# A clamp moved from VectorE to GpSimd, waits of GpSimd for VectorE's weight rounding, and another written-out order, in a fused set attention and SwiGLU kernel

## The chip, the cores and the metric

The kernel runs on one core of a Trainium2 chip. The metric is the device time of one execution in microseconds (us). Of several executions the median is taken. One further execution was profiled; its own time is given beside the others. The engines are named as in the profile: PE is TensorE (matrix products), PEld its weight load, DVE is VectorE, ACT is ScalarE, POOL is GpSimd, and SP is the queue that issues most DMAs.

## The reference

The reference is an attention block followed by a gated feed-forward block, all in float32.

```python
# x: (4, 12416, 128)   inducing: (32, 128)
def mab(q, kv):
    s = scale * (q @ kv.transpose(0, 2, 1))
    s = s - s.max(-1, keepdims=True)
    a = np.exp(s)
    a /= a.sum(-1, keepdims=True) + 1e-09
    return a @ kv
h = mab(inducing, x)        # 32 rows a batch
x = mab(x, h)               # 12416 rows a batch
# x as 49664 rows of 128; w_gate, w_val: (128, 1536), w_out: (1536, 128)
rms = np.sqrt(np.mean(x * x, axis=-1, keepdims=True) + 1e-06)
xn = x / rms * rms_g
g = xn @ w_gate
out = (g / (1 + np.exp(-g)) * (xn @ w_val)) @ w_out
```

The three weight matrices come as float64 words in DRAM and are turned into float32 on the chip.

## The kernel before

**Units and blocks.** Each of the 4 batches is cut into 25 units of mostly 512 tokens (some of 480, one of 256). A unit passes through 12 blocks of 128 hidden features, so there are 1200 blocks. A block is a gate product on PE (`gate`, L709), a Silu on ACT (`silu`, L719), a value product on PE (`value`, L737), and a product of the two on DVE (`times_value`, L751). Then the block is projected with `w_out` into a sum in PSUM.

**Three sorts of projection.** A written-out string gives each block a sort. Sort P multiplies the float32 factor directly (`project_plain`, L807: two matmul records a block). Sorts S and D split the factor into a high and a low part, so that three faster products do (`project_two`, L795 and L796, and `project_third`, L807). In sort S, ACT makes the high part (`high`, L764), DVE the low part (`low`, L770) and POOL their sum (`add_in_place`, L815). In sort D, ACT makes the high part (L761), POOL the low part (`low_of_u`, L777), ACT scales the high part (L783), and POOL makes the sum (L815). Before the change 368 blocks are P, 635 S and 197 D.

**Attention beside it.** While the blocks of one batch run, the scores, exponentials and sums of the next one are computed in small steps between them. The rows of a batch are also normed (`norm`): a transpose on DVE (L548), a small product (L562, L569), a product (L574) and a sum of rows on DVE (`scale`, L583), which gives the mean squares `ms`; then `clamp` (L586), a maximum of `ms` and 1e-6 over 8 to 64 numbers a partition; then a first guess of the inverse root on ACT (`seed`, L590), and three rounds of a root iteration, each with two steps on ACT (L594, L600) and two on POOL (L597, L603); then the product of the weights with it on POOL (L608). There are 10 such clamps in the part of the kernel described here. The first set of rows has its own code ahead of it, with its own clamp (L1029) and root (L1032), which the change does not touch.

**Rounding of the weights.** Each of nine chunks of 128 x 512 weights is turned from float64 words into float32 by four DVE steps: `power` (L226) and `upper` (L239), each a shift or mask of one operand in SBUF, and `sign` (L248) and `lower` (L254), each with two operands in SBUF. Two ACT steps lie between (L204, L206), and `join` on POOL (L260) multiplies the parts. Some of these steps run in the opening (`first`, a written-out order of its own), the others among the first blocks, next to the splitting of `w_out` (L666 to L672 on ACT and POOL).

**The order.** Every engine runs its instructions in the order in which the program emits them. That order is a string, `program`, with one letter a step (g, s, v, m for the parts of a block, h, l, n, e, q, d, r, p for its projection), and a dot for one of 871 steps of attention, norm and rounding, whose number is read from a second list, `taken`. Further strings give the PSUM bank (`banks`), the buffers (`workers`, `outputs`, `holders`), the block's sort (`sorts`), and which of several waiting blocks goes next (`picks`). The layer below adds the waits that the data need.

```python
    for name in "".join(program.split()):
        if name == ".":
            step, args = micros[int(next(taken))]
            step(*args)
        else:
            do[name]()
```

Of the kernel before, what the change touches and what calls it, by code (L numbers as in the profile page):

```python
# [14 lines left out]
ALU = mybir.AluOpType  # L15
# [8 lines left out]
def kernel(  # L24
# [501 lines left out]
    def norm(b, sets):  # L526
# [58 lines left out]
        def clamp():  # L585
            nc.vector.tensor_scalar(out=st["ms"], in0=st["ms"], scalar1=1e-6, scalar2=None, op0=ALU.max)  # L586
# [595 lines left out]
    def seams():  # L1182
# [61 lines left out]
        gpmdojlkhqiasncrlpmekqsnobgfjpmrlkdaqsionmrljchekpofnqgsmrkplojbsmnqrkplodajsrcknmqiopjlsknrhmqjflnsebropjgdklan
        msrqocpjikhflqonmpsjrklgmqeopnsdrbalkcjmhiqnsfoprlkqgnsjdoemkaqprlnsjcmonskbrlfqphjmoniasrkqlpjodkgmnseclfbjprko
        qhmsinrlkjpomdgcnljqakrbopesmfjhopincabsmjkqolrndgsmjpfqhelaknbosrmcjqplikrmnjqogpdhfkslrjmanoqpblekcjgrmnsfqljp
        iokqdnhrlsjamopnkqergfcslmjbophankridmqojepslnkromfcgdplkbrsnqjopakhrifclmsngjqeoprkdbljmqsnrokpmaclfijrhgqosnkj
        pmdrlsnqebckorpjmslikqnrhafopjslmkgdqcebnorjlpmsqkniafhldopcmrsjqgnkelobmprqfsljnokhmadpsiglrcbjqefdg
    """
    sorts = """  # L1250
        PPPPPDPPPPPPDPDDPPPSPDDPDPPPDPPDDPPPPPPSSSSDPPDPDPDPPDPSDPPSPSPSSSDPDPPPPSSDSPSDDSSPSSSSDPSSSSSSPSSDPSPSSSSDDSPS
        DSDPSPSSPSSSSSPSDDPSPDSPPDPSPSSPPSPPSSSDDPSPPSSSPDSPSSSDSSPSSSSPSSPSSSSSSSDSDPSPSSPDSDSSPSSSSDSDSDSSSPSPSSPSDSDP
        PPPPSSDSSSSPDPSPSSSSDDPSPPPSPDPDDSPPSDSPPDSSDPPPSPSPPSSSSSPPPPSSDPPSSDDDPPPPDPDDPDPSSDPSPSPDDPSSSPPPSPSSSDDPPPSD
        PSSSDPSPDSPSSPSDSDDSSSPSSSSDDPSPSSSPPSSDDPSSPPSSPDSSSSDSSSPSSPSDPSDSPSPSSSSSDSPSDSSPSSSSSDPPPSSPDSSDPPDSPSPPSPPS
        SDDSPPSSDSSPDPSSSSSDSSPSSSSSPPSSSSSDSSPSSSSSSPSSSDSPSSSSSSDSSSDPSSSSPDSSPDSPSSSPSSDPSSSPSSDPSSPSDPSSPSSPPDSPDDPP
        PPSPDDSPSSSSPSPSPSPPSSPDSPSPPSSPSDSSSPSPDDDPDPSDPSPSDPPSPDSPSDPPSPPSSSDPSPSSSSDSDPSPSPSSSDDSSDPSPSDSSSSPDPDPSSPP
        SDSDSPSSPSPSDSSSPPSSPDSSDDSDPSSSSPDSPSSSSDSSPSSPSSDSPPSPSSSSSDPPDPSDDPPPSPSSPSSDSDPPDSSDPSSSSPSSDSSPPSDSPSSSSSSS
        SDSPSSSPDSSDSSSSSSSDPSSDSSDPSPSSSSPSSSDPPSSPSSSSSSPDSSSPPSDDSSPSDSPPPDPDDPDPPPPPDPDPSSPSSPSPSSPSDPSPPPSPPPPSSSSD
        PSSPSDSSDPSSDPPSDSPSSSSDPSPPSSPSSPPSPSSSPSSSSDSSSSPSSSDSSSSSPSSSPSPSDDSSPSPSPSSSSSSSSPDSDPPSPSSSSSPSSSDSSSSSSSPS
        SSPDSPSSSPSSDSSPSSPSPSSSSDSSDPSPSPSSPSSSSSSDSPSSPSDSSPSPSSSSSPDSSPSSPSSSSSSDSPSSSSPSSSDDPSSPPSPSDSPSSSSSSDPSSSSS  # L1260
        SPDSSPPSSSSSSSSSDSPPSPSSSSDSPSPSSSDSSPSSSSSPSDPSSSSPDPSSPSSSSPSDSSPSSPSPPDPDPPPP
    """
# [225 lines left out]
```

## Time and profile before

| what | value |
|---|---|
| median of three executions | 1492.43 us |
| lowest and highest | 1492.39 and 1493.38 us |
| the profiled execution's own time | 1493.58 us |
| its span in the profile | 1491.8 us |
| granted TensorE clock | 1.00 |

The span is what the profile shows from the first to the last instruction. Busy times of an engine's instructions are merged where they overlap. Matmul ends are modelled, so the distance from one matmul to the next tells more of the pace than its duration.

### The profile page before, as it was taken

How to read it: one execution, taken by the hardware profiler on the slowest of the kernel's cores; microseconds unless marked ns; L12 is line 12 of the kernel's file. 1: busy time of each engine (PE TensorE's matmuls, PEld its weight loads, DVE VectorE, ACT ScalarE, POOL GpSimd, SP SyncE). 2: the span in 40 equal slices, each digit the busy share in tenths (PEclk: the TensorE clock that was granted, in tenths of full speed). 3: DMA queues.
4: the chain of work that ended last, by engine and by line, in shares of the span. 5: the costliest groups of instructions: out<-in, count | busy, mean ns of one | idle time of the engine just before them, and what ended most of it. 6: DMA issues, size and time to landing. Idle time of an engine off the chain costs nothing.

```text
span 1491.8 us, 25915 instructions
## 1 busy us (share of the span) xinstructions
PE 1471.9 (99%) x7280; PEld 1100.2 (74%) x7280; DVE 1431.6 (96%) x2471; ACT 1308.5 (88%) x2603; POOL 1372.0 (92%) x1190
## 2 busy tenths in 40 slices
PE   8899999999999999999999999999999999999998
PEld 6456777767777777777777777777767777787787
DVE  6999998999999999899999999999999999999998
ACT  5798889888988888988999888998898889898987
POOL 1588997999999999899999999989989999999998
PEclk9999999999999999999999999999999999999999
DMA  7576324438553313445755312263332121222122
GB/s 285 113 117 112 64 40 97 87 94 125 101 92 66 57 31 70 87 94 125 118 104 103 74 29 43 43 134 86 76 63 45 29 40 36 42 40 41 36 42 35
DMA packets 391712, 116.28 MB, mean 78 GB/s; under 512 B 365584, under 2 KB 370704, under 8 KB 389008
## 3 DMA queue, kind: packets, MB, share of 16 engines
q1 hardware_dynamic: 390976, 114.55, 39.4%
q8 instruction: 58, 0.95, 0.3%
q14 instruction: 86, 0.70, 0.2%
q10 hardware_dynamic: 592, 0.08, 0.0%
HBM read 53.95 MB, written 27.00 MB: 54 GB/s over the span
## 4 chain that ended last, share of the span: by engine, by line
PE 93%; DVE 3%; issue 1%; ACT 1%; DMA 1%; SPq 0%; POOL 0%; DVEq 0%; ACTq 0%; POOLq 0%
PE gv L807 31%; PE gv L737 17%; PE gv L709 17%; PE gv L795 12%; PE gv L796 12%; PE gv L316 3%; PE gv L369 1%; DVE u L751 1%; PE gv L908 1%; DMA xn<-in_x_dram 1%; PE gv L569 1%; DVE o L254 0%; DVE we L248 0%; DVE we L226 0%; DVE gv L751 0%
## 5 line engine op out<-in xcount | busy, mean ns | idle before, releaser
L719 ACT ACTIVATE silu<-gv 128x512 f32<-128x512 f32 (+2 forms) x1200 | 670.6, 593 | 87.1 <-PE gv L709 61.5
L815 POOL TENSOR_TENSOR xn<-xn,xn 128x512 fp32r<-128x512 f32 (+1 forms) x480 | 596.1, 1259 | 17.0 <-PE gv L796 13.5
L709 PE MATMUL gv<-a,sg 128*128 128x512 f32 (+2 forms) x1188 | 490.8, 440 | 3.8 <-DVE xn L770 1.8
L737 PE MATMUL gv<-a,sv 128*128 128x512 f32 (+2 forms) x1188 | 442.8, 408 | 1.5 <-DVE sv L492 1.0
L751 DVE TENSOR_TENSOR gv<-silu,gv 128x512 f32<-128x512 f32 (+2 forms) x635 | 417.4, 677 | 9.6 <-ACT silu L719 4.5
L764 ACT ACTIVATE xn<-gv 128x512 fp32r<-128x512 f32 (+1 forms) x616 | 362.1, 599 | 38.1 <-DVE gv L751 31.1
L751 DVE TENSOR_TENSOR u<-silu,gv 128x512 f32<-128x512 f32 (+2 forms) x565 | 360.9, 655 | 13.2 <-ACT silu L719 5.9
L807 PE MATMUL gv<-u,wo 128*128 128x512 f32 (+2 forms) x736 | 361.3, 575 | 3.1 <-DVE u L751 3.1
L770 DVE SCALAR_TENSOR_TENSOR xn<-xn,gv 128x512 fp32r<-128x512 f32 (+2 forms) x516 | 337.7, 666 | 6.5 <-ACT xn L764 4.6
L709 PEld LDWEIGHTS gv<-a,sg 128*128 128x128 f32 x1188 | 223.2, 189 | 114.7 <-issue 35.1
L737 PEld LDWEIGHTS gv<-a,sv 128*128 128x128 f32 x1188 | 222.9, 189 | 90.5 <-issue 25.1
L815 POOL TENSOR_TENSOR xn<-xn 128x512 fp32r<-128x512 f32 (+2 forms) x201 | 251.7, 1259 | 12.7 <-PE gv L796 9.8
L777 POOL TENSOR_TENSOR xn<-u,xn 128x512 fp32r<-128x512 f32 (+2 forms) x165 | 206.5, 1257 | 21.5 <-ACT xn L761 19.0
L815 POOL TENSOR_TENSOR u<-xn,u 128x512 fp32r<-128x512 f32 (+2 forms) x131 | 162.9, 1248 | 5.3 <-PE gv L796 2.6
L795 PE MATMUL gv<-xn,xn 128*128 128x512 f32 (+2 forms) x439 | 167.7, 382 | 0.0
L807 PEld LDWEIGHTS gv<-u,wo 128*128 128x128 f32 x736 | 137.0, 190 | 27.0 <-issue 9.6
L807 PE MATMUL gv<-xn,xn 128*128 128x512 f32 (+2 forms) x367 | 141.0, 390 | 0.0
L796 PE MATMUL gv<-xn,xn 128*128 128x512 f32 (+2 forms) x367 | 137.5, 375 | 0.0
L795 PE MATMUL gv<-xn,more 128*128 128x512 f32 (+2 forms) x349 | 135.0, 387 | 0.0
L783 ACT ACTIVATE xn<-xn 128x512 fp32r<-128x512 f32 (+2 forms) x196 | 122.4, 632 | 7.5 <-POOL xn L777 6.4
L761 ACT ACTIVATE xn<-u 128x512 fp32r<-128x512 f32 (+2 forms) x196 | 122.4, 626 | 7.5 <-DVE u L751 5.6
L807 PE MATMUL gv<-xn,more 128*128 128x512 f32 (+2 forms) x302 | 114.7, 391 | 0.0
(223 smaller groups left out, 1818.9 us busy)
## 6 DMA issues: line engine op xcount, KB each, us to landing
out_dram<-o SPq DMA_DIRECT2D x320, 64.0 KB, 2.0
xT<-in_x_dram SPq DMA_DIRECT2D x60, 256.0 KB, 4.9
xn<-in_x_dram SPq DMA_DIRECT2D x60, 256.0 KB, 5.4
a<-hi SPq DMA_DIRECT2D x156, 64.0 KB, 2.0
a<-lo SPq DMA_DIRECT2D x156, 64.0 KB, 2.0
xn<-in_x_dram SPq DMA_DIRECT2D x5, 1024.0 KB, 9.7
xn<-w SPq DMA_DIRECT2D x18, 256.0 KB, 3.8
out_dram<-o SPq DMA_DIRECT2D x64, 60.0 KB, 2.0
```

What stands on the lines that cost most here:

```text
L709: nc.tensor.matmul(g[:, 0:T], stacks[b][0][:, ts(j, P)], halves_in_turn(one["a"][:, 0:T]), start=True, stop=True)
L719: nc.scalar.activation(sl[:, 0:T], gates.pop(n)[:, 0:T], AF.Silu)
L737: nc.tensor.matmul(v[:, 0:T], stacks[b][1][:, ts(j, P)], halves_in_turn(one["a"][:, 0:T]), start=True, stop=True)
L751: nc.vector.tensor_tensor(out=to, in0=sl[:, 0:T], in1=v[:, 0:T], op=ALU.mult)
L761: nc.scalar.activation(hi, t["u"], AF.Copy, scale=1.0 - 2.0 ** -13)
L764: nc.scalar.activation(hi, t["u"], AF.Copy, scale=-(1.0 - 2.0 ** -13) * 2.0 ** -12)
L770: nc.vector.scalar_tensor_tensor(out=t["lo"], in0=t["hi"].bitcast(F32), scalar=4096.0, in1=t["u"], op0=ALU.mult, op1=ALU.add)
L777: nc.gpsimd.tensor_tensor(out=t["lo"], in0=t["u"], in1=t["hi"].bitcast(F32), op=ALU.subtract)
L795: nc.tensor.matmul(to, weight_of(0, j), halves_in_turn(t["hi"]), start=not one["q"], stop=False)
L796: nc.tensor.matmul(to, weight_of(1, j), halves_in_turn(t["lo"]), start=False, stop=last)
L807: nc.tensor.matmul(to.rearrange("p (n h) -> p h n", h=2) if step2 else to, lhsT, rhs, start=one["left"] == NJ, stop=one["left"] == 1)
L815: nc.gpsimd.tensor_tensor(out=t["lo"], in0=t["hi"].bitcast(F32), in1=t["lo"].bitcast(F32), op=ALU.add)
```

## The change

It has three parts.

- The clamp of `norm` (L586) is issued to GpSimd in place of VectorE.
- While the order is emitted, each DVE step of the rounding (`power`, `upper`, `sign`, `lower`) is remembered, and the next GpSimd instruction that is emitted is made to wait for the last of them.
- All the order strings are new: `program`, `taken`, `banks`, `workers`, `outputs`, `holders`, `sorts`, `picks`. The number of blocks and of the 871 small steps is the same. The sorts are now 362 P, 643 S and 195 D. `first` and its order are as before.

```diff
         def clamp():
-            nc.vector.tensor_scalar(out=st["ms"], in0=st["ms"], scalar1=1e-6, scalar2=None, op0=ALU.max)
+            nc.gpsimd.tensor_scalar(out=st["ms"], in0=st["ms"], scalar1=1e-6, scalar2=None, op0=ALU.max)
...
     sorts = """
-        PPPPPDPPPPPPDPDDPPPSPDDPDPPPDPPDDPPPPPPSSSSDPPDPDPDPPDPSDPPSPSPSSSDPDPPPPSSDSPSDDSSPSSSSDPSSSSSSPSSDPSPSSSSDDSPS
+        PPPPPPPPPPPPPDDDPPPSPDPPDPPDPDPSSDPPDPDPPDPPPPPSDDDPDPDPSPSPSDPDSSPPPPSSPSSSSDSPSDPSSPDSSSSSSSDPSPSDDPSSPSPSDPSD
...
+    held = None
+    alone = {id(one[name]) for one in weight.values() for name in ("power", "upper", "sign", "lower")}
     for name in "".join(program.split()):
-        if name == ".":
-            step, args = micros[int(next(taken))]
-            step(*args)
-        else:
-            do[name]()
+        made = len(nc.cur_bb.bb.instructions)
+        step, args = micros[int(next(taken))] if name == "." else (do[name], ())
+        step(*args)
+        one = nc.cur_bb.bb.instructions[-1]
+        if id(step) in alone:
+            held = one
+        elif held is not None and one.engine == mybir.EngineType.Pool and len(nc.cur_bb.bb.instructions) > made:
+            tc.add_manual_dep(one, held.name, mybir.DependencyInfo(mybir.DependencyClass.Sync, mybir.DependencyReason.DATA),
+                              reason="no two at the shared port")
+            held = None
```

More of the change, by code (lines that the diff above doesn't have):

```diff
@@ new lines @@
+        7426543172632516730257156701350357064317064306247604062475027064571427015701537414213547231472513467541350463150
+        4135046530241564363016430176301746301724630716207516205321056310261405631574316371536741670456306751067102652057
+        2570126507142571245714235174271354270643276345276527346275327464152364526345324502643056413206415027561207561057
+        6120376253172142674561426541270564217045720437142741037126407236257342653475367264157637164314017360713604137607
+        4153756345315215634160254310523104571230451204750416205421602364013503052413547032451724657142637162314761234712
@@ new lines @@
+        3467123061421325614532426756053075620562357230167501653176417534675671362457214235120321370157312510367250617564
+        6246041712160421736230173616071561637601563075643764532645234256325143521463251305402503254234720472536420736027
+        3464167462061270416071521050616521063215031025463152603176031635071736051630154702432124157134512745163721641206
+        4236143613260413670326470260237052670325710263517253237543154713273561247623407636270612071023610256751467251462
+        5176514725641357613615617036710536057167102571271470254724107521460152403514325431423014250145301504305450370457
@@ new lines @@
+        6302456730245632431206523026312560712037614261013071437201357240153425304614620136014620132014327345207354037540
+        2354673046215406215046510265402650264765072673250632753604327453715052054517420714756210425601352103210650263501
+        7653145075065351375061750537215403140537120142307203142031643127532654512435625142305364502347052367327642576324
+        7321437250437524375240732605413251427141346124361724173062413602410536140351406351436547065203405306524502340267
+        3402640230634026413062167403641036401351463514056734256741265243124631623562041354163257435731516547635016741571
@@ new lines @@
+        2056215625460216452130420643274320436076204753264357614213471362376423016720472014564152420641205340263275602475
+        2760574025176254637251372457143152307451204715276510761026517365023640576042734350423754210753702132370210726135
+        2071362073462130143061402134561042615067156215427546172534526134063456145601634507645174607462071274126702671347
+        0360135017673617536072361251725374327341534752362145362341301503520450137243031702310612067032613760521705620412
+        7405170124073517354014607436746574053764052364721307063710726317503274052374062032764271603274026703653627620756
@@ L1245 @@
[L1245 to L1248, printed above, removed]
+        abcdefghiabdcejkflmgnohibapqdrscefhgljibmkedpqnorscalhgfbmjiednkcgorfabdpsieqlmocgnpafrshkjdbqlimonregqlcspmoakj
@@ new lines @@
+        fhdqlbspnimrqkolesjgpncmraqdohfkiblsmpnojrqkmelnspgcjqaromsblhdfkpnjroicqmlgasnerkbplojqmfsdrhqnkaplmogbsrikjpql
+        ncmofesrkjdhpmlnaqogbcisrdkjlnepmhqkjolnpmfjosabrlnpcmjdoqgkhrlnpsoemjikrlnfqpbcsmjoldaqkspnmrjlqgoknhesicprfmlo
+        qjnkspdormbgjeknqpslomjqrhaksonpfirlmjcqdobnrekpmshjqgloanikfrjpmslqndokrsbjlcpmeqohgnkraifpmsjbcelqhondgkrsjpml
+        oqnikfcbpralsemjhgdoqcbkpenrlmsjfgoqkpalmisjnorkdqplmbhcnroqklefgsmpjaknilrdohqsbcmefpgadicjkafnliropqbsmjkcdnrp
+        lfoqghasmeijkbncrpdfglohiqsjmebakngqsrpfjmdchiloegknfqsbrpkcajnqlsodrmpkqgiljhnsapbcdermokqnsplhaojkrqfgsnlmojkr
@@ new lines @@
+        dpqiblmcsnekroajslngmphqkorfdljcnqbkmspliornjqkemlsporangqhdfieskjmbciopaqldrnjmshrfnjqslgcbaokeprnqimljsdonkqph
+        fcrmlobkqgnjaspedrmfhncigbjlokqsrmepnjlqsrmpnqodkscrmjlbqhokaspniefqrgmjlospkqdnclbosmhkanroqmpejsglkfonqrmlipch
+        jsdoknqrmpjlboksrmnlapoegsqkjmrlposkqjmfnrlpoihkjcbaqlsmepndokgrjfsqhomrljkcpnisqoramljbekpsnfdqogrmhjlkpscqaieb
+        jkglrpofsncqmhijkaedpoblsgrncqjfhmkpiabrnelmpgfqsjkordplmnqjahombckpnsirqefjlgkdpnahsormbckqejplnrsigfdkojqampcr
+        lbesnhjqfkmiopdrlsnajqckmoprgbejlhsniqrokpmjsfdlacqneprmjgoshlbifcqnkmpjrodslagkqnmipjsherlckoqpfjnbmsrdkgaljqok
@@ new lines @@
+        pinmecrsfljhakpgqbinodcmrslqkjneposfalqhmkbgrjdcenspmokifrjalpqmohbnlgersipjkqomnfrcbpsdjkglohqmrnjpkeloasqbmrnj
+        pgcfklosinjmqahrpdecbgikladmqnofijrhbcspgklmqaednfoklspjrmnohqklpbicsjrqknmlorkpnsqgjmefoklrnpqhjdoabslikmcqjfrn
+        pokqmgsjlrponmkqsjlrpondkslbhjmerpqnikasloqcnkjfghesldrnpomkqjsbcalpmokhqrsnjlikpemqdrfgcosnbkjamoilphqredgsnfbk
+        jclpmoqrsnakjilpmoqrhsedfmnlobkpgcajqrslomnikphfloersdmnjqckprlsmojgbnqaifkpojhsrlmedcgnqsobaifhkjedglmcrpsnqklo
+        bjmfrpeqsaknildgcjmoqhsknlbrfapoiqjrmskneplcoqjdrmskgnphljofqrbmsaknplojiqrcmeskodpjnmgblqfsrokpjnhsrmolkapqnjsi
@@ new lines @@
+        SSDSSSSSPSDSPSSPPSSPSPDDPPDPSPSSPSDSSSDSPSDPSSPSSSPSDSSPPSDSPSSSSSSDPSSPDSSSSSSSPSSSSSSSSDSDPSSSSDPSSPSPSSSSSSSP
+        PSDDDSPPSSPDPPSPPSDSSSSPDPSPDPDPSDPPSSPSPSSPDSSSPSPPSSPSPPSPSSPSPDSDPDPPPDPPSSDPSSDDDPDPPPSSDPDPSPPSPPSPSDDDPPPS
+        PDPSPSDSSDSSSPDDPDPSSSSSPSSDSSSDDPPSPSSSSDPSSPSDPPSSSSSSDSSPSSSDPSPDPDSPSSSSSSSSDPSSSPSPSSSDDPSDPDPPSPPPSDSSSDSS
+        SSSDPSSPSSDPSPDSSSSPSSSSSSSSDPSPSSDSPPSSSSSSSSSSSSSSSSSSDSSSPPDPSDSPSPDPSSSSPSPSSDSDPSPDSSPSSSSDSPSDPDPPPSPDSDPS
+        PPSPDSDPSSSSPSSPPSDPSSPPPSSPSPPSSPPSSDSSDPSDDPSDPSPPSSDSPSSPSPSPSPSDSSDPSPSPSDDPPDSSSSDPPSSPSDSDSPPSSSDSSDDPSPPD
@@ new lines @@
+        SPSPPDSSSSPSDDDPPPDSSDPSPSSSDSPSSSSSDPSDSPSSSSDSSPSSDPSDDPPSPPSPSDPDDPPSPDPPSPSSSSSSDSPSSSSSSSSSPSDSSSSDSPSPSPSS
+        SSSSSSSSSSSSDDSSPSSDSSPSDSSSSPPSSSSSSDSDPSSPPSDSDPDPPSPPPSSSSSDSPSSPPDSSPDPPSSSDDPSPSPSSPSSSPSPPPPSSSDPPPPSSDDPP
+        PSPSDSSSDPSPDDPPSSDSSPPSSPSSSSSPSSSSPSPSSPSSDSPSSPSSSSPDSPSSSSSSPSSSDSSPSSPSSSSDPSSPPSSSSSDSDSPSPSSSPSSSDSSSPSPS
+        SSSDSPSSPSSSDPSSSSPSSSSPSSDDPSPSSSSPSSSSSDSSPPSSSPSSSDSSPSSPSSSDSDPSPSSPSSSPSSSSSSSSDPSSPSSDSPSPSPSSSDSPSSSPSSSS
+        SSDPSPSSPSSSSDSSSPSPSSDSSPSSSSPSDSPDSPSSSSPSSSSSSPDPSSSPSSPDSSPSSSSSPSPDPDPDPPPP
@@ new lines @@
+        AAABACAABAAAAAAAAAAAAAAAAAAAAAAAAAAAAAAAAAAAACABAAAAAAAAAAAAAAAAAAAAABCACACAAAABAAAAABAAAAAAAAAAAAAAAAAAAAAAAAAA
+        AAAAAAAAAAAAAAABAAAAAABAAAAAAAACAAAABAAAAAAAAAAAAAAAAAAAAACABBAAAAAAACABAAAAABAAAAAAAAAAABBAAAAABAAAAAAAAAAAAAAA
+        AAAAAAAAAAABAAACAAABAAAAAAAAAAAAAAAAACABAAAAAAAAAAAAAABAAAAAAAABBAABBBAAAAAABBAAAAAAAAAAAAAAAAAABBBAABAABAAAAAAA
+        CAACABAABAAAAAAAAAAAAAAAABAAAAAAACABAABAABBAAAAAABAAAAAAAAAAAAAAAAAAAAAAAAAAAABAAAAAABAAAAAABAAAAAAAAAAAAAAAAAAA
+        AAAAAABAAAACABAAAAAAAAAAAAAAAABAAAAAAAAAAAABAAAABABAAAAAAAAABAAAAAAAAAAAAAAAABAABABAAABAAAAAABAAAAAAAAAAAAAAAAAA
@@ new lines @@
+        AAAAAABAAAAAAAAAAAAACAAABAAAAAAAAAAAABAAAAAAAAAAAAAAAABBAAAAAAAAAAAAAAAAAAABAAAAABBBAAAAAABAAABCAAABAAAAAAAAAAAA
+        AAAAAAAABAAAAAAAAAAAAAABBAAAAAAABAAAAABABAAAAAABAAAAAAABAAAAAAAAAAAAAAAAAAAAABAABAAAAAAAAAAAAAABAAAAAABAAAAAAAAA
+        AAAAAAAAAAAAAAAAAAAAAAAAAAAAAAAAAABABAAAAAAAAABAAAABABAAAAAAAABBAAAAAAAAAAAAAAAAAAAAAAAAAAAAAAAAAAAAAAAAAAAAAAAA
+        AAAAAAAAAAAAAAAABAAAAAAAAAABAAAAAACAAAAAAAAAAAAAAAAAAAAAAAAAAAAAAAAAAAAAAABABABAAAAABAAAABAAAABBAAAAAAAAAAAAAAAA
+        AAAAAAAAAAAAAAAAAAAAAAAAAAAAAAACAAAAABAAAAAAAAAAAAAAAABAAAAAAAAAAAAACAAAAAABAAAAAAAAAAAAAAAAAAAAABAAAAAAAAAAAAAB
@@ new lines @@
+        ABAAAAABAAAAABAAABAAAACAAAAAAAAAAAAAAAAAAAAAAAAAAAAABAACAAAAAAAAAABAAAAAAABAAAAAAAAAABAAAAAAAAAAAAAABAAAAAAAAAAA
+        ACAAAACAAAAAAABAAAAAAAAAAABBAAAAAAAAAABAAAAAAAAAAAAAAAAAAAAAAAAAAAABAAAAAAAAAAAAABAABAAAAAAAAAAAAAAABAAABAAAAAAA
+        AAAAAAAAAAAAABAAAAAAAAAAAAAABAAAAAAAAABAAAAAAAABAAAAAAAAAAAAABAAAAABAAAAAAAAABABAAAAAABAAACAAAAAAAACAAAAAAABBABA
+        AAAACAAAAAAAAAAAAABAAAAAAAAAAAABBAAAAAABAAAAAAABAAAAAAAAAAAAAAAAAAAAAAAAAAAAAABAAAAAABAAABAAAAAAAAACAAAAAAAABAAA
+        AAAAAAAAAAAAAAAAAAABAAAAAABAAAAAAAAAAABAAAAAABBAAAAAAAAAAAAAAAAAAAAAAABAABAAAAAAAAAAAAAAAABABAAABAAAAAAAAABAAABA
@@ new lines @@
+        DCAAAAAAAAAAAAAABAAAAAABAAAAAAAAAAAAAAAAAAAAAAAAABBAAAAABAABAAAAAAAAAAAAAAAAAABABAAAAAAAAAAABAAAAAAAAAAAAAAAAAAB
+        AAAAAAAAAAABAABAAAAAAAAACABCAAAAAAAAAAAAAAAAAAAAAAACAABABAAAAAABAAAAAABAAAAAAAAAAAAAAAAAAAAABAAAAAAABAAAAAAAAAAA
+        AAAAAAAAAAAAAAAAAAAAAAAAAAAAAAAAAAAAAAABAAAAAAAAAAAABABAAAAAAAAAAAAAABAAACAACABAACAAABAAAAAAAAAAAAAAAAAAAAAAAAAA
+        AAAAAAAAAAAAAAAAAAAAAAAAAAAAAACAAABAAAAAACABAAAAAABAAADBCBAAAAAAAAAAAAAAABAABAAAAAAAAAAAAAABAAAABCAAAAAAAAABAAAA
+        AAAACABABAAAABAABAAAAAAAAAAAAAAAAAAAAAABACAAABAAAAAAAAAAABBAABAAAAAAAAAAAAAAAAAABAAABAAAAAAAAAAAAAAAAAAAAAABAAAA
@@ L1407 @@
+        pmhsvlrnrhrmgvsqldgermvsvFgdhqmgsvqlsdvhrmrglgqhdrmspslhdgvmvsqlvrhgdqmsqlgrmdspmhTgvvdsqlOmrEgmqgrsdghvrsmvpsmh
+        gnvpsmgvnevrmsgvFphdsvgmeqnpmsTqdrepmOpdqpEdprrrFTO
     """
     taken = """
[30 rows of a table removed]
[30 rows of a table added]
         867 868 869 870
```

324 lines of the change are left out of this document (130 added, 194 removed), and 60 rows, old and new, of the table taken.

## The prediction

> **What bounds the kernel now.** I read the page first, then busy times by stage, then the chain of waits by stage. The page gives the span, the busy time of each engine, and the costliest groups.
>
> ```profile
> span 1491.8 us, 25915 instructions
> PE 1471.9 (99%) x7280; PEld 1100.2 (74%) x7280; DVE 1431.6 (96%) x2471; ACT 1308.5 (88%) x2603; POOL 1372.0 (92%) x1190
> L815 POOL TENSOR_TENSOR xn<-xn,xn 128x512 fp32r<-128x512 f32 (+1 forms) x480 | 596.1, 1259 | 17.0 <-PE gv L796 13.5
> L764 ACT ACTIVATE xn<-gv 128x512 fp32r<-128x512 f32 (+1 forms) x616 | 362.1, 599 | 38.1 <-DVE gv L751 31.1
> L770 DVE SCALAR_TENSOR_TENSOR xn<-xn,gv 128x512 fp32r<-128x512 f32 (+2 forms) x516 | 337.7, 666 | 6.5 <-ACT xn L764 4.6
> ```
>
> Four engines are nearly full, so a share of the span does not say which one ends it. The busy times by stage (opening code, first blocks with weight rounding, the long middle with attention beside the blocks, the last batch) say more.
>
> ```profile
> 0.00:44.00 44.00, 39.47 (x444) 29.04 (x444) 30.10 (x92) 24.14 (x52) 8.83 (x18) 1.00 0.69 254
> 44.00:80.00 36.00, 29.27 (x101) 15.22 (x100) 35.30 (x51) 26.84 (x52) 20.46 (x17) 1.00 0.61 117
> 80.00:1150.20 1070.20, 1068.26 (x5277) 790.01 (x5277) 1034.31 (x1768) 957.07 (x1901) 1012.77 (x879) 1.00 0.44 82
> 1150.20:1492.00 341.80, 334.90 (x1464) 265.90 (x1462) 331.92 (x564) 300.45 (x601) 329.92 (x279) 1.00 0.22 39
> ```
>
> The columns are length, then busy us (and count) of PE, PEld, DVE, ACT and POOL, then clock, DMA share and GB/s. From 44 to 80 us DVE is busy for 35.30 of 36 us, while PE has 6.7 us and POOL 15.5 us free. After 80 us DVE is free for 35.9 and 9.9 us. The chain of waits agrees. In the stretch of 44 to 80 us it runs mainly over DVE, rounding steps among them; after 80 us it runs over PE. The two lines are those two stretches.
>
> ```profile
> by line: DVE u L751 23.0%; issue 15.2%; DVE o L254 12.5%; DVE we L226 7.6%; DVE we L248 7.2%; DVE sg L492 5.8%; PE gv L737 5.2%; DVE o L239 4.6%; PE gv L709 4.3%; DVE sv L492 3.9%; PE gv L316 2.8%; PE gv L152 2.5%; PE gv L1054 2.1%; DVE sc
> by line: PE gv L807 32.4%; PE gv L737 17.6%; PE gv L709 17.6%; PE gv L795 12.2%; PE gv L796 12.2%; PE gv L316 2.3%; PE gv L369 1.2%; issue 0.7%; PE gv L569 0.5%; DVE gv L751 0.3%; PE gv L463 0.2%; SPq L557 0.2%; DVE u L751 0.2%; DMA xn<-xn
> ```
>
> So a microsecond taken from DVE before 80 us is a microsecond of the end. After 80 us it counts only where a late DVE has emptied PE.
>
> **The rounding steps, 44 to 80 us.** For L226, L239, L248 and L254 in this order, busy DVE time and count, first in a stretch in which POOL does little, then among the blocks:
>
> ```profile
> 10.00:46.00 36.00, 2.11 (x5) 1.00 0.63 226
> 47.00:78.00 31.00, 3.32 (x4) 1.00 0.70 136
> ...
> 10.00:46.00 36.00, 1.66 (x4) 1.00 0.63 226
> 47.00:78.00 31.00, 3.01 (x4) 1.00 0.70 136
> ...
> 10.00:46.00 36.00, 2.05 (x3) 1.00 0.63 226
> 47.00:78.00 31.00, 6.74 (x6) 1.00 0.70 136
> ...
> 10.00:46.00 36.00, 2.03 (x3) 1.00 0.63 226
> 47.00:78.00 31.00, 6.19 (x6) 1.00 0.70 136
> ```
>
> Quiet, they take 0.42, 0.42, 0.68 and 0.68 us each. For 4, 4, 6 and 6 of them that is 1.7 + 1.7 + 4.1 + 4.1 = 11.5 us. They took 3.3 + 3.0 + 6.7 + 6.2 = 19.3 us, so 7.8 us were lost beside POOL. The new wait keeps the next POOL instruction in the order from starting until the rounding step is done. It does not hold back the POOL instruction ahead of it. The worst overrun shows the two starting within 0.02 us:
>
> ```profile
> 75.82 1.28 POOL L777 TENSOR_TENSOR xn<-u,xn 128x512 fp32r<-128x512 f32 x1 [0.20 <-ACT xn L761]
> 75.84 1.81 DVE L254 SCALAR_TENSOR_TENSOR o<-sg,o 128x512 f32<-128x512 uint32 x1
> ```
>
> Whether such a pair is parted depends on which of them stands first in the new order. I take half of 7.8: **-3.9 us** (bounds 0 and -7.8). In the order of the changed kernel about five POOL instructions get a wait that they had no reason for (L668 and L672 of the `w_out` splitting, one L445); the others after rounding steps are joins (L260) that wait for such a step anyway. Behind these five on POOL stand joins and the first sums (L777, L815), and PE's stacks of weights wait for the joins. POOL's 15.5 free us cover them: 0 us, and at most 5 x 1.26 = 6.3 us, one sum's length each, if the cover is gone.
>
> **The clamps.** All ten of L586 on DVE in one row, then the longest with what POOL and the chain of waits did (start, us), and three more places where a clamp lies on the chain or PE's timeline shows the gap behind it:
>
> ```profile
> 78.00:1492.00 1414.00, 10.44 (x10) 1.00 0.38 71
> ...
> 320.05 3.85 DVE L586 TENSOR_SCALAR ms<-ms 128x15 f32<-128x15 f32 x1
> 318.84 3.80 POOL L815 TENSOR_TENSOR u<-xn,u 128x512 fp32r<-128x512 f32 x3
> 322.55 1.32 POOL L777 TENSOR_TENSOR xn<-u,xn 128x512 fp32r<-128x512 f32 x1
> 320.97 2.84 issue
> ...
> 443.17 1.18 DVE xn L586
> 803.18 0.92 issue
> 1174.53 0.48 PE L709 MATMUL gv<-a,sg 128*128 128x512 f32 x1 [1.79 <-DVE xn L770]
> ```
>
> A clamp of 15 numbers a partition held DVE for 3.85 us, until the fourth of a row of POOL instructions was done. The chain lost 2.84 us there, 1.18 at 443 us, 0.92 at 803 us and 1.79 at 1174 us: 6.7 us. All of it goes when DVE no longer clamps: **-6.7 us** (bounds 0, if something else is late right behind, and -10.4, the whole row).
>
> The Trainium skill ("SBUF — State Buffer", section "SBUF: two separate sides") calls the pair of ports that DVE and GpSimd share an exclusive lock, given for the whole instruction to whichever starts first. By that rule the clamp at 320.05 us would have started as soon as the sum running then ended; three further POOL instructions passed it, so the trace shows a dearer lock than the page. By the page the ten clamps would have cost DVE an estimated 3 to 4 us, and this term would be about 3 us.
>
> What the clamp costs on POOL no row shows. The nearest are the root steps of the same tiles on POOL, the widest and the narrowest:
>
> ```profile
> L597 POOL TENSOR_TENSOR xn<-xn 128x64 f32<-128x64 f32 x9 | 2.8, 315 | 0.6 <-ACT xn L594 0.6
> L597 POOL TENSOR_TENSOR rt<-rt,ms 32x8 f32<-32x8 f32 x3 | 0.6, 192 | 2.1 <-ACT rt L594 2.1
> ```
>
> Ten at 0.19 to 0.32 us are 2 to 3 us of POOL. POOL is free for 57.4 us in the middle and 11.9 us in the last stage, which covers them: **0 us** on the path. What POOL's wait ahead of a clamp may cost is the second rival.
>
> **The sorts.** Six blocks go from P to a split sort; S grows by 8, D falls by 2. PE's pace from the chain of waits:
>
> ```profile
> 707.69 0.86 PE gv L807 x2
> 711.56 0.22 PE gv L795
> ```
>
> A P block takes 0.86 us of PE, a split one 3 x 0.22 = 0.65 us. Six times 0.21 is **-1.3 us**, all on PE, which is the chain after 80 us. DVE gains 8 low parts of 0.67: +5.3 us. POOL gains 6 sums and loses 2 lows: 4 x 1.26 = +5.0 us. ACT gains 4 x 0.60 = +2.4 us, of which 183 free us take no notice. Of DVE's 5.3 I charge half, **+2.7 us** (bounds 0 and 5.3), since DVE has 45.8 us free after 80 us but is often the one that is waited for.
>
> **The order itself.** Everything is moved: every engine's sequence and SP's loads and stores differ. In the opening stretch SP issues the same gathers, weight loads and first loads of the next batch in nearly the same places, so I cost its moves at nothing; DMA's share of 0.61 there covers them. For the rest, the trace has two long stretches with the same work in different orders, the gates of blocks 301 to 600 and 601 to 900:
>
> ```profile
> 431.10:790.70 359.60, 124.53 (x300) 1.00 0.44 83
> 790.70:1150.20 359.50, 123.28 (x301) 1.00 0.35 69
> ```
>
> They took 359.6 and 359.5 us. Two orders of one kind differ little, so a new one counts as 0 here, with an estimated +-1 us a batch.
>
> **The sum.** -3.9 - 6.7 + 0 - 1.3 + 2.7 = -9.2 us. The profiled execution's own time was 1493.58 us, so it becomes 1484.4. It lay 1.15 us over the median of 1492.43, so the forecast for the median is **1483.2 us**. With the far bounds its own range is about 1475 (-7.8 - 10.4 - 1.3 + 0 = -19.5 would be 1473) to 1489.
>
> **Rivals.**
>
> *The gain of the clamps is only handed on (1490 us).* After 80 us the chain is PE's. Where DVE is no longer late, another wait may come up at the same place: the stall at 320 us has such a tail, shown by the chain of waits:
>
> ```profile
> 327.15 1.29 POOL xn L777
> 328.46 0.63 ACT xn L783
> ```
>
> Until 329 us POOL and ACT were late there too. Then the 6.7 us go, and 1492.4 - 3.9 - 1.3 + 2.7 = 1489.9 remains. The gap of 1.79 us ahead of PE at 1174 us, with DVE named, speaks against it. The Trainium skill ("Perfetto Trace Analysis", section "Optimizing Scalar/DVE Operations") warns that moving work between GpSimd and DVE might not help because they share a port.
>
> *The added waits miss the pairs (1487 us).* If each overrun of the rounding is with a POOL instruction that stands ahead in the order, the opening loses its 3.9 us of gain: 1483.2 + 3.9 = 1487.1. The pair at 75.8 us, nearly simultaneous, allows it; still faster.
>
> *POOL's queue becomes the late one (1502 us).* A clamp at the head of POOL's queue waits for DVE's row sum (L583), and behind it stand the sums (L815) that PE's third product needs. The nearest row is the untouched first root, for which POOL waited on DVE's clamp:
>
> ```profile
> 40.82 3.26 POOL L1032 TENSOR_TENSOR rs<-ms,rt 128x8 f32<-128x8 f32 x2 [3.73 <-DVE ms L1029]
> ```
>
> At half of 3.73 us for each of ten clamps, with no cover, it is 18.7 us: 1483.2 + 18.7 = 1501.9. It turns the result to slower than before from 1.2 us a clamp (9.2 + 3.0 over ten). For it speaks that POOL is busy for 329.92 of 341.8 us in the last stage and gains 7 to 8 us of work in all; against it, that DVE, now less delayed, makes the sums earlier.
>
> **How the numbers follow.** A difference of 0.2%, 3.0 us, is about what a measurement can tell from none, so faster means under 1489.4 and slower over 1495.4. Chances: forecast 0.58, missed pairs 0.12, both faster, 0.70; handed on 0.11, which is no change; POOL's queue 0.19, slower. The range of 1475 to 1498 holds the forecast with nearly all its bounds, both faster cases, the handed-on case, and the milder part of POOL's queue.
>
> **What would show each step.** L586 appears under POOL, at 0.2 to 0.35 us each, and no DVE instruction of 8 to 64 numbers lasts over 0.7 us. The 20 rounding steps of the flow take near 15 us, or 11.5 if all pairs are parted, and the last is done about 4 us earlier than at 77.7 us. The middle and last stages show no PE gap of over 1 us with a norm step's DVE neighbour named. I am wrong if L597 or L815 on POOL wait longer for DVE than before, if POOL's new waits push the joins and PE's stacks late, or if 300 blocks of the middle take more than 360 us.

## The result, and the profile after

The changed kernel took 1481.65 us (median of four, 1481.31 to 1481.77), against 1492.91 us for the kernel before in the same series (four, 1492.39 to 1495.92). The ratio is 0.992, with a 95% interval of 0.9903 to 0.9937. The forecast was 1483.2 us, with a range of 1475 to 1498.

The page's first lines and the busy times of the last three of the four stages answer to those of before. The second stage ends shortly after the last rounding step, and the third where block 900 is done (columns as before: length, then PE, PEld, DVE, ACT, POOL).

```profile
span 1479.7 us, 26001 instructions
PE 1467.6 (99%) x7286; PEld 1102.4 (74%) x7286; DVE 1420.0 (96%) x2469; ACT 1309.5 (88%) x2605; POOL 1378.8 (93%) x1204
...
44.00:74.00 30.00, 27.40 (x99) 14.33 (x98) 28.48 (x50) 23.17 (x45) 14.49 (x12) 1.00 0.71 140
74.00:1139.30 1065.30, 1064.70 (x5279) 791.47 (x5275) 1030.80 (x1764) 958.39 (x1906) 1023.80 (x894) 1.00 0.44 82
1139.30:1480.00 340.70, 335.34 (x1472) 266.62 (x1470) 330.61 (x566) 303.90 (x605) 331.54 (x282) 1.00 0.22 39
```

DVE's busy time fell by 11.6 us, from 1431.6 to 1420.0. The steps of the prediction give the same: 10.4 for the clamps, plus 6.7 for the rounding steps (below), less 5.3 for eight more low parts, is 11.8. POOL's busy time rose by 6.8 us, against a forecast of 7 to 8.

Where along the run the time went is seen from the gates on PE, each row some 300 blocks:

```profile
421.90:781.00 359.10, 122.04 (x302) 1.00 0.45 85
781.00:1140.10 359.10, 122.88 (x302) 1.00 0.35 69
1140.10:1480.00 339.90, 118.30 (x300) 1.00 0.22 39
```

The gates of the first 300 blocks were through at 421.9 us in place of 431.1: 9.2 us of the 12.1 between the two profiled executions were won by then. The two middle batches won 0.5 and 0.4 us, and the last one about 2.

**The rounding steps.** Busy DVE time and count of L226, L239, L248 and L254 among the blocks, and the last of them:

```profile
46.30:90.00 43.70, 1.84 (x4) 1.00 0.74 137
46.30:90.00 43.70, 2.13 (x5) 1.00 0.74 137
46.30:90.00 43.70, 4.43 (x6) 1.00 0.74 137
46.30:90.00 43.70, 4.33 (x6) 1.00 0.74 137
...
69.94 0.71 DVE L254 SCALAR_TENSOR_TENSOR o<-sg,o 128x512 f32<-128x512 uint32 x1
```

The second row's fifth is the last 0.1 us of a step of the opening. So the 20 steps took 12.6 us in place of 19.3, near the 11.5 of quiet ones, and the last ended at 70.65 us in place of 77.65.

**The clamps** are on POOL, ten of them, 3.1 us in all. The last number of a row is POOL's idle time before them:

```profile
L586 POOL TENSOR_SCALAR xn<-xn 128x64 f32<-128x64 f32 (+2 forms) x7 | 2.4, 338 | 2.1 <-DVE xn L583 1.6
L586 POOL TENSOR_SCALAR ms<-ms 128x16 f32<-128x16 f32 (+2 forms) x3 | 0.7, 243 | 0.3
```

In PE's groups after 80 us, the rows whose idle time (the last number) is over 0.1 us are only these two. In the same view of the kernel before, L709 had 2.1 us, of which 1.8 with DVE's L770 named, and L316 had 1.1.

```profile
L737 PE MATMUL gv<-a,sv 128*128 128x512 f32 (+2 forms) x1169 | 441.4, 410 | 0.3 <-ACT silu L719 0.2
L807 PE MATMUL gv<-xn,xn 128*128 128x512 f32 (+2 forms) x363 | 135.0, 383 | 0.5 <-POOL xn L815 0.3
```

### The profile page after: what moved, and what is told of

Read it like the earlier page. It is cut to its first block, busy times and chain, and to the rows that moved or that the text cites. A ratio compares the mean times of both kernels' runs of the same rounds, so it can differ in the third digit from the quotient of the medians.

```text
span 1479.7 us, 26001 instructions
## 1 busy us (share of the span) xinstructions
PE 1467.6 (99%) x7286; PEld 1102.4 (74%) x7286; DVE 1420.0 (96%) x2469; ACT 1309.5 (88%) x2605; POOL 1378.8 (93%) x1204
## 4 chain that ended last, share of the span: by engine, by line
PE 94%; DVE 2%; DMA 1%; issue 1%; ACT 1%; POOL 0%; SPq 0%; DVEq 0%; ACTq 0%; POOLq 0%
PE gv L807 31%; PE gv L709 17%; PE gv L737 17%; PE gv L795 12%; PE gv L796 12%; PE gv L316 3%; PE gv L369 1%; PE gv L908 1%; DMA xn<-in_x_dram 1%; DVE u L751 0%; PE gv L569 0%; DMA xT<-in_x_dram 0%; PE gv L463 0%; DVE o L239 0%; DVE we L248 0%
## 5 line engine op out<-in xcount | busy, mean ns | idle before, releaser
L815 POOL TENSOR_TENSOR xn<-xn,xn 128x512 fp32r<-128x512 f32 (+2 forms) x486 | 605.0, 1264 | 15.5 <-PE gv L796 14.0
L709 PE MATMUL gv<-a,sg 128*128 128x512 f32 (+2 forms) x1188 | 482.1, 431 | 0.6 <-DMA a<-lo 0.6
L764 ACT ACTIVATE xn<-gv 128x512 fp32r<-128x512 f32 (+1 forms) x629 | 370.0, 598 | 32.9 <-DVE gv L751 27.0
L807 PE MATMUL gv<-u,wo 128*128 128x512 f32 (+2 forms) x724 | 353.5, 573 | 1.1 <-DVE u L751 1.0
L770 DVE SCALAR_TENSOR_TENSOR xn<-xn,gv 128x512 fp32r<-128x512 f32 (+1 forms) x516 | 337.4, 664 | 8.9 <-ACT xn L764 6.2
L709 PEld LDWEIGHTS gv<-a,sg 128*128 128x128 f32 x1188 | 223.3, 189 | 106.6 <-issue 32.4
L815 POOL TENSOR_TENSOR xn<-xn 128x512 fp32r<-128x512 f32 (+1 forms) x204 | 255.3, 1257 | 7.0 <-PE gv L796 4.0
L777 POOL TENSOR_TENSOR xn<-u,xn 128x512 fp32r<-128x512 f32 (+2 forms) x174 | 218.2, 1260 | 15.7 <-ACT xn L761 15.2
L795 PE MATMUL gv<-xn,xn 128*128 128x512 f32 (+1 forms) x441 | 169.7, 385 | 0.0
L795 PE MATMUL gv<-xn,more 128*128 128x512 f32 (+2 forms) x355 | 137.6, 388 | 0.0
L796 PE MATMUL gv<-xn,xn 128*128 128x512 f32 (+2 forms) x363 | 135.9, 374 | 0.0
L807 PE MATMUL gv<-xn,xn 128*128 128x512 f32 (+2 forms) x363 | 135.0, 383 | 0.5 <-POOL xn L815 0.3
L807 PE MATMUL gv<-xn,more 128*128 128x512 f32 (+2 forms) x311 | 118.8, 396 | 0.0
```

Of the source, the lines that this page charges most:

```text
L709: nc.tensor.matmul(g[:, 0:T], stacks[b][0][:, ts(j, P)], halves_in_turn(one["a"][:, 0:T]), start=True, stop=True)
L764: nc.scalar.activation(hi, t["u"], AF.Copy, scale=-(1.0 - 2.0 ** -13) * 2.0 ** -12)
L770: nc.vector.scalar_tensor_tensor(out=t["lo"], in0=t["hi"].bitcast(F32), scalar=4096.0, in1=t["u"], op0=ALU.mult, op1=ALU.add)
L777: nc.gpsimd.tensor_tensor(out=t["lo"], in0=t["u"], in1=t["hi"].bitcast(F32), op=ALU.subtract)
L795: nc.tensor.matmul(to, weight_of(0, j), halves_in_turn(t["hi"]), start=not one["q"], stop=False)
L796: nc.tensor.matmul(to, weight_of(1, j), halves_in_turn(t["lo"]), start=False, stop=last)
```

## The experiments

Two theories were held against each other: that the gain is the contention of DVE and POOL which the two local edits take away, and that it is the new order as such. All times are medians. Each is compared with the kernel before in its own series: 1492.91 us for the changed kernel, 1492.54 for e1 to e4, 1491.95 for e5 to e8 and 1492.25 for e9 to e11. The last three series ran on three different chips.

| run | order | clamps | waits | median, us | to before | ratio (95%) |
|---|---|---|---|---|---|---|
| changed kernel | new | POOL | yes | 1481.65 | -11.3 | 0.992 (0.9903 to 0.9937) |
| e1 | new | DVE | yes | 1487.49 | -5.1 | 0.9958 (0.9944 to 0.9971) |
| e2 | new | POOL | no | 1482.59 | -10.0 | 0.9929 (0.9916 to 0.9941) |
| e3 | old | POOL | no | 1489.58 | -3.0 | 0.9978 (0.9969 to 0.9986) |
| e4 | old | DVE | yes | 1491.00 | -1.5 | 0.9987 (0.9978 to 0.9995) |
| e5 | old | POOL | yes | 1488.52 | -3.4 | 0.9978 (0.9969 to 0.9987) |
| e6 | new | DVE | no | 1488.83 | -3.1 | 0.9975 (0.9966 to 0.9985) |
| e7 | old | none | no | 1485.63 | -6.3 | 0.9955 (0.9943 to 0.9968) |
| e8 | old | DVE, other form | no | 1486.20 | -5.8 | 0.9962 (0.9948 to 0.9975) |
| e9 | new | DVE, other form | yes | 1480.00 | -12.3 | 0.9917 (0.9903 to 0.9931) |
| e10 | new | none | yes | 1479.47 | -12.8 | 0.9913 (0.9900 to 0.9927) |
| e11 | old | DVE, other form | yes | 1485.64 | -6.6 | 0.9953 (0.9940 to 0.9967) |

**e1: the clamps back on VectorE, in the new order.**

```diff
-            nc.gpsimd.tensor_scalar(out=st["ms"], in0=st["ms"], scalar1=1e-6, scalar2=None, op0=ALU.max)
+            nc.vector.tensor_scalar(out=st["ms"], in0=st["ms"], scalar1=1e-6, scalar2=None, op0=ALU.max)
```

> The changed kernel with the clamps of norm back on VectorE, order and waits kept. Theory (the clamps lose time to GpSimd's back-to-back instructions at a port that the two share): of ten clamps three or four last 1 us or more on VectorE, and the time goes up by about 6.7 us, to 1488 (1485 to 1490, since it depends on the order which ones collide). Rival (the new order as such makes the gain): the clamps cost their own 0.2 us each, 1482 to 1483.

It gave back 6 of the 11 us, and four of the ten clamps lasted over 1 us, both as the theory had it. The worst clamp in the timelines of DVE, POOL and PE:

```profile
380.90 3.91 DVE L586 TENSOR_SCALAR ms<-ms 32x8 f32<-32x8 f32 x1
380.57 0.60 POOL L445 TENSOR_TENSOR sc<-sc,mx 32x256 f32<-32x256 f32 x1
381.13 0.19 POOL L292 MEMSET gram<- 128x128 f32 x1
381.29 1.19 POOL L815 TENSOR_TENSOR xn<-xn,xn 128x480 fp32r<-128x480 f32 x1
382.45 2.34 POOL L815 TENSOR_TENSOR xn<-xn 128x480 fp32r<-128x480 f32 x2
385.46 0.50 PE L709 MATMUL gv<-a,sg 128*128 128x480 f32 x1 [2.70 <-DVE xn L574]
```

Eight numbers on 32 partitions held DVE for 3.91 us, until POOL paused after five instructions, and PE stood for 2.70 us. In the kernel before this same clamp took 0.15 us, and the one of 15 numbers 3.85: which one is hit depends on the order, and in both orders some are.

**e2: no added waits, in the new order.**

```diff
-            tc.add_manual_dep(one, held.name, ..., reason="no two at the shared port")
             held = None
```

> The changed kernel without the added waits of GpSimd for the rounding steps; order and clamps kept. Theory: some of the rounding steps meet a GpSimd instruction again and take 1.3 to 1.8 us; of the 6 to 7 us of overrun that went, 2 to 6 come back: 1484 to 1488. Rival (the order alone keeps them apart): no change, 1481.7, rounding steps still about 13 us in all.

The rival was nearly right: about 1 us comes back (1.3 by the table), and the two intervals overlap over most of their length, so the times alone do not show it. The trace does show some loss: the rounding steps take 14.3 us in place of 12.6. The new order keeps most of them apart even without its waits.

**e3: only the clamps moved, in the old order.**

```diff
-            nc.vector.tensor_scalar(out=st["ms"], in0=st["ms"], scalar1=1e-6, scalar2=None, op0=ALU.max)
+            nc.gpsimd.tensor_scalar(out=st["ms"], in0=st["ms"], scalar1=1e-6, scalar2=None, op0=ALU.max)
```

> The kernel before with only the clamps moved to GpSimd. Theory: the 6.7 us that the chain of waits lost at 320, 443, 803 and 1174 us go, 1486 (1484 to 1488). Rival (they are only handed on to another wait at the same place, since the order was made for clamps on VectorE): 1491 to 1494. Second rival (GpSimd's queue waits for the row sums at each clamp): 1497 to 1502.

The gain was 3.0 us, between the theory and the rival of a gain that is handed on. The timelines show one way in which it was handed on: the row sum on DVE, POOL's instructions ahead of the clamp, the clamp, the guess on ACT, and PE.

```profile
757.32 1.23 DVE L583 TRANSPOSE_TENSOR_REDUCE xn<-xn 128x32 f32<-128x1024 f32 x1
758.88 1.20 POOL L777 TENSOR_TENSOR xn<-u,xn 128x480 fp32r<-128x480 f32 x1 [0.34 <-ACT xn L761]
760.04 1.21 POOL L815 TENSOR_TENSOR xn<-xn,xn 128x480 fp32r<-128x480 f32 x1
761.34 0.36 POOL L586 TENSOR_SCALAR xn<-xn 128x64 f32<-128x64 f32 x1
761.73 0.26 ACT L590 ACTIVATE xn<-xn 128x64 int32<-128x64 int32 x1 [1.02 <-POOL xn L586]
762.59 0.44 PE L807 MATMUL gv<-xn,xn 128*128 128x480 f32 x1 [0.64 <-ACT xn L594]
```

The row sum was ready at 758.55 us; the clamp ran 2.79 us later, behind POOL's queue. ACT, whose next instruction was the guess, stood for 1.02 us, and PE then stood for 0.64 us, with a root step on ACT named. The same clamp in the changed kernel:

```profile
750.18 1.23 DVE L583 TRANSPOSE_TENSOR_REDUCE xn<-xn 128x32 f32<-128x1024 f32 x1
752.79 0.37 POOL L586 TENSOR_SCALAR xn<-xn 128x64 f32<-128x64 f32 x1
755.06 0.28 ACT L590 ACTIVATE xn<-xn 128x64 int32<-128x64 int32 x1
```

Here it ran 1.38 us after the sum, and the guess came later in ACT's order, so ACT did not wait. Over the ten clamps the delay was 0.1 to 3.05 us in the old order (seven of ten over 1.5) and 0.1 to 1.4 in the new. A delay is no loss by itself: the longest, of 3.05 us at 1166 us, left PE without a gap. ACT's idle time ahead of the guesses (the last numbers), first in e3, then in the changed kernel:

```profile
L590 ACT ACTIVATE xn<-xn 128x64 int32<-128x64 int32 (+2 forms) x7 | 1.8, 260 | 3.4 <-POOL xn L586 3.4
L590 ACT ACTIVATE rs<-ms 128x16 int32<-128x16 int32 (+2 forms) x3 | 0.7, 233 | 0.9 <-POOL ms L586 0.9
...
L590 ACT ACTIVATE xn<-xn 128x64 int32<-128x64 int32 (+2 forms) x7 | 1.7, 243 | 1.3 <-POOL xn L586 1.3
L590 ACT ACTIVATE rs<-ms 128x16 int32<-128x16 int32 (+2 forms) x3 | 0.7, 233 | 0.4 <-POOL ms L586 0.4
```

That is 4.3 us against 1.7. That the loss runs over ACT is read from these rows; no run moved the guess alone.

**e4: only the waits added, in the old order.**

```diff
+        elif held is not None and one.engine == mybir.EngineType.Pool and len(nc.cur_bb.bb.instructions) > made:
+            tc.add_manual_dep(one, held.name, ..., reason="no two at the shared port")
```

> The kernel before with only the added waits of GpSimd for the rounding steps. Theory: half of the 7.8 us of overrun goes, 1489 (1486 to 1491). Rival one (each overrun is with a GpSimd instruction ahead in the order, which the wait does not hold): 1492 to 1493, overruns unchanged. Rival two (GpSimd, waiting, is late for the joins): 1494 to 1497.

A gain of 1.5 us, between the theory (3.5) and rival one (none). The steps of the four kinds, in the order L226, L239, L248, L254:

```profile
46.30:90.00 43.70, 2.57 (x4) 1.00 0.71 126
46.30:90.00 43.70, 2.15 (x4) 1.00 0.71 126
46.30:90.00 43.70, 5.89 (x6) 1.00 0.71 126
46.30:90.00 43.70, 6.83 (x6) 1.00 0.71 126
```

They still take 17.4 us of 19.3, so a quarter of the overrun is gone. The five steps that still overran by 0.7 us or more each began 0.2 to 0.5 us after a POOL instruction had started, and the wait holds back only the next one.

**e5: both edits, in the old order; e6: the new order with neither.**

```diff
 e5:  the edits of e3 and e4 in the kernel before
 e6:  the edits of e1 and e2 in the changed kernel
```

> The kernel before with both local edits, the clamps on GpSimd and the waits of GpSimd for the rounding steps, in its old order. If the two add, 1492.5 - 3.0 - 1.5 = 1488.0; the 6.4 us that are then left to 1481.65 belong to the new order. Rival (the two edits make up the whole change and only need each other): 1481 to 1484.

> The new order alone: the changed kernel with the clamps back on VectorE and without the added waits. If the losses add, 1481.65 + 5.8 + 0.9 = 1488.4, still 4 us under the kernel before: that is what the order itself brings. Rival (the order is worth nothing without its rule): 1491 to 1494.

The edits bring 3.4 us in the old order (1488.52 us, against 1488.0 if they added), and the new order, its sorts with it, 3.1 us without them (1488.83, against 1488.4 if the losses of e1 and e2 added); together they bring 11.3. About 5 us are there only where both are. The first theory alone and the second alone are both too small. e1 and e3 show why on the side of the clamps: in the new order clamps on DVE collide again, and in the old order clamps on POOL come late.

**e7: no clamps at all, in the old order; e8: the clamps on VectorE in another form.**

```diff
 e7:
-            nc.vector.tensor_scalar(out=st["ms"], in0=st["ms"], scalar1=1e-6, scalar2=None, op0=ALU.max)
+            pass
 e8:
-            nc.vector.tensor_scalar(out=st["ms"], in0=st["ms"], scalar1=1e-6, scalar2=None, op0=ALU.max)
+            unused = small.tile([P, 1], F32, name="tiny")[rows, :]
+            nc.vector.tensor_scalar(out=st["ms"], in0=st["ms"], scalar1=1e-6, scalar2=None, op0=ALU.max, op1=ALU.max,
+                                    accum_out=unused)
```

> The kernel before with the ten clamps of norm left out (the maximum with 1e-6 is not taken), nothing in their place. It is the floor for what a cheaper clamp can bring in the old order. Theory (what the clamp cost was VectorE's wait at the port, and a clamp on GpSimd is nearly free): the same as with the clamps on GpSimd, 1489 to 1490. Rival (the clamp on GpSimd delays the root behind GpSimd's queue and gives back half of the gain): 1485 to 1487.

> The kernel before with the clamps still on VectorE, but in the form that also writes out a maximum over the row into a spare number (one more instruction each). Theory (the plain form waits for a port that GpSimd holds, this form does not use it): each clamp takes 0.2 to 0.3 us with the second instruction, none over 0.5, and the time is that with the clamps on GpSimd, 1489 to 1490. Rival (any VectorE instruction of this size is held up behind GpSimd): again clamps of 1 to 4 us, 1492 to 1494.

Without clamps the old order gains 6.3 us. So the clamps were worth what the chain of waits said, and the clamps on POOL cost 3.4 of it. In e8 the clamp of 15 numbers, which had taken 3.85 us, stood between the same two POOL sums (these lines are numbered two higher in this kernel):

```profile
318.94 0.15 DVE L587 TENSOR_SCALAR_CACHE_REDUCE ms<-ms 128x15 f32<-128x15 f32 x1
319.02 0.08 DVE L587 DVE_READ_ACCUMULATOR ms<-ms 128x1 f32 x1
317.82 2.52 POOL L817 TENSOR_TENSOR u<-xn,u 128x512 fp32r<-128x512 f32 x2
```

With POOL busy all the while, it took 0.15 us, and 0.08 for the second instruction. The time was that of no clamps within 0.6 us. The places agree too. In the profiled executions the gates of e8 ran 1.1 us ahead of those of before at block 150, 4.0 at 250, 4.8 at 350, 5.6 at 650 and 7.9 at 950: steps of 2.9, 0.9, 0.8 and 2.3 us, where the prediction had priced clamps at 2.84, 1.18, 0.92 and 1.79. (Half of the second step came at two clamps before that of 443 us.) ACT stood for 0.3 us ahead of the guesses, against 4.3 in e3. So it was the form of the instruction that made it wait, not the engine's work. The Trainium skill ("SBUF — State Buffer", section "Who interferes with whom") names `tensor_scalar` among those that can take the shared ports, and excepts the form that also writes out its accumulator; these rows agree.

**e9, e10 and e11: what is left.**

```diff
 e9:   the clamp of e8 in the changed kernel
 e10:  the clamp of e7 in the changed kernel
 e11:  the clamp of e8 and the waits of e4 in the kernel before
```

> The changed kernel with its clamps on VectorE in the form that also writes out a maximum; order and waits kept. In the old order this form beat GpSimd's by 3.4 us, because GpSimd's clamp there ran 1.5 to 3 us after the row sum it needs. In the new order GpSimd's clamp runs 0.4 to 1.4 us after it. If what the old order lost was that delay, little is left to gain: 1480 to 1482. Rival (GpSimd's work or its queue is what a clamp costs in any order): 1478 to 1479.

> The changed kernel with the ten clamps of norm left out (the maximum with 1e-6 is not taken): the floor for a cheaper clamp in the new order. First reading: 1480 to 1481.5. Rival: 1478 to 1479.

> The kernel before, old order, with the clamps on VectorE in the form that also writes out a maximum, and the waits of GpSimd for the rounding steps. If the two add in the old order, 1486.2 - 1.5 = 1484.7, about 3 us over the changed kernel: that is then what the new order brings beyond both edits at their best (mostly the rounding steps that it keeps apart). Rival (the waits bring nothing here): 1486.

In the new order the clamps on POOL cost 1 to 1.5 us by the table (e10, at 1479.47 us between its two expectations), not 3.4. That lies inside the intervals, but the traces bear it out: the gates of e9 run ahead of the changed kernel's by 0.3 to 0.5 us more at each of the clamps of 753, 792 and 1113 us, and by 1.6 for most of the last batch. The wait of ACT is not the reason here: it stood for 1.9 us ahead of the guesses in e9 and for 1.7 in the changed kernel. What the reason is stays open.

The median of e9 is the lowest of all kernels that compute everything, 1480.00 us; but its ratio of 0.9917 and the changed kernel's 0.992, taken in different series, lie well inside each other's intervals, so that it beats the changed kernel is not shown by the times. The waits of e11 add 0.8 us to the gain of e8, which is inside the intervals and nearer the rival of no gain.

e11 and e9 say what the new order is worth beyond both edits at their best: 12.3 - 6.6 = 5.7 us. In the two profiled executions e9 is 1.6 us ahead at the first gate, 5.8 at block 300 and 6.9 at the end, so most of it comes from the first 300 blocks. There the rounding steps are kept apart, which saves 4.8 us of DVE (17.4 to 12.6 us) in the stage in which the chain ran over DVE; an estimated 1.3 us is PE's share of the six sorts by its pace. No run parts the two.

## Why the prediction was right

- **The bounds by stage: right.** Most of the gain, 9.2 of 12.1 us, lies in the first 300 blocks, where the DVE-bound opening and the longest clamp are. The middle batches, paced by PE, won half a microsecond each, the estimated +-1.
- **The rounding steps (-3.9): too small.** The overrun shrank by 6.7 us, from 7.8 to 1.1, and the last step came 7.0 us earlier. The step that failed was to credit this to the waits and halve it. In the old order the waits took 1.9 us of overrun (e4) and brought 1.5 us; in the new order their absence cost about 1 us (e2). The rival of missed pairs was right on the waits, and the order did what they could not. The trace of before had it already: the eight steps that overran by 0.4 us or more, 7.2 of the 7.8 us, all began 0.01 to 1.1 us after a POOL instruction had started.
- **The price of the added waits (0): not contradicted.** POOL stood for 4.2 us in all ahead of L668, L672 and L445 with a rounding step named, and one L672 of 1.27 us lies on the chain of waits; but without the waits the kernel was not faster (e2).
- **The clamps off VectorE (-6.7): right.** e7 measured 6.3 us, and the gates of e8 show the gain at the four places that were named.
- **The clamp on POOL (0): right by luck of the order.** It cost 3.4 us in the old order and 1 to 1.5 in the new. Not POOL's work was dear (3.1 us in all, forecast 2 to 3, and the same in both orders), but the place of the clamp in its queue. POOL's free 57 us were no cover for that: the cover of a busy total says nothing of the delay of one instruction.
- **POOL's queue as the late one (1502): the right place, the wrong way round.** POOL hardly stood waiting for DVE's row sums: it was idle for 2.4 us before the ten clamps of the changed kernel, 1.6 of them with a row sum named. The row sums waited for POOL. A single clamp ran up to 3.05 us late in the old order, more than the 1.87 us that the prediction took for each, but most of that was covered: ten clamps cost 3.4 us and not 18.7.
- **The sorts (-1.3 and +2.7): not measured apart.** Buffers and order hang on the sorts. DVE's and POOL's busy times moved as counted. With the rounding at -6.7 in place of -3.9, the sum is -12.0; measured were -11.3. So the charge of 2.7 and the PE term are not contradicted, and not shown.
- **The order (0): wrong as a single term.** Alone it brought 3.1 us (e6), and together with the edits 5 us more than the parts. A new order that is made together with edits cannot be costed beside them as one more term.
- **The number: partly luck.** The forecast gave the whole gain to the two edits, -3.9 - 6.7 = -10.6 us, and nothing to the order. The edits brought 3.4 us in the old order and 7.2 in the new (1488.83 to 1481.65). What they lacked, the order made up.
- **The forecast's own range (to 1489): its upper end does not follow.** With the far bounds of its terms on that side, 0, 0, -1.3 and +5.3, it ends at about 1496. The result lies inside either.

## What to carry to other kernels

A tiny VectorE instruction can cost as much as several large GpSimd ones if its form uses the ports that both share: look at the longest, not the mean, of each small group, and lay GpSimd's timeline beside it. Before moving such an instruction to GpSimd, try another form on VectorE; here, without a change of the order, it brought 5.8 of the 6.3 us that leaving the clamps out brings, where the move brought 3.0. In a program whose order is fixed, an instruction that changes its engine needs a new place in the queue: the two edits brought 3.4 us in the old order and 7.2 in the new one. A wait that is added helps only if the instruction that it holds is the one that collides, and here most collisions were with the one ahead.

## What the runs showed of the hardware that was not expected

In these runs a VectorE instruction that waited for GpSimd was not let in when the running GpSimd instruction ended: in e1 one of 32 x 8 numbers was passed by a memset and three sums and took 3.91 us, and one of 128 x 15 in the kernel before took 3.85 us behind four sums and differences. The same clamp that also writes out a maximum took 0.15 us beside the same GpSimd sums. The Trainium skill ("SBUF — State Buffer", section "SBUF: two separate sides") says that whichever starts first gets the shared ports for the whole instruction; in these two rows VectorE was let in only after four further GpSimd instructions in e1 and three in the kernel before, so GpSimd in effect kept the ports over a row of instructions.
